# Retention, ELU feed-forward and gated feed-forward on one core: heads' halves exchanged in every second pair of the last nine retention steps

## The chip, the core and the metric

The kernel runs on one core of one Trainium2 chip, in one launch. The metric is the device time of the launch in microseconds, as the median of several runs. The engines are TensorE (PE: matmuls, with its weight loads as PEld), VectorE (DVE), ScalarE (ACT), GpSimd (POOL) and SyncE (SP, which here issues nearly all DMAs). Their programs run side by side, each strictly in its own order, and wait for each other through semaphores.

## What is computed

All data is float32. A retention (attention with a decaying causal mask and no softmax) over 4 batches, 8 heads, 576 positions and a head size of 64 is followed by two feed-forward layers over its 2304 tokens of 512 features:

```python
def _attn_ref(q, k, v):
    scores = scale * np.matmul(q, k.transpose(0, 1, 3, 2))       # scale = 1/8
    gamma = 1.0 - 2.0 ** (-5.0 - np.arange(H))
    rel = pos[:, None] - pos[None, :]
    Dmat = np.where(rel >= 0, gamma[:, None, None] ** rel, 0.0)
    return np.matmul(scores * Dmat, v)

def _moe_ref(x, w_in, w_out):
    h = x @ w_in
    return np.where(h > 0.0, h, np.exp(np.minimum(h, 0.0)) - 1.0) @ w_out

def _moe2_ref(x, w_gate, w_val, w_out):
    gate = 1.0 / (1.0 + np.exp(-(x @ w_gate)))
    return (gate * (x @ w_val)) @ w_out
```

## The kernel before

The retention runs in chunks of 128 positions: 18 steps, numbered n = 0 to 17. Steps 0 to 8 belong to batches 0 and 1, steps 9 to 17 to batches 2 and 3; within nine, the two batches take turns, and the ninth (8 and 17) does the last 64 positions of both. A step has 4 pairs of heads (p). In q and in the transposed k of a pair, head h = 0 lies on partitions 0 to 63 and head h = 1 on 64 to 127, and so does its state, the decayed sum of k times v over all earlier chunks. A chunk has two halves of 64 positions, X = 0 and 1.

TensorE's array is used in quarters of 64x64: the rows come from the partitions of the operands (upper or lower half), the columns go to the partitions of the result. A step issues five kinds of 64x64x64 matmuls, all through `mm` (L263), into two pairs of PSUM banks, `ts` and `to`:

- `scores`: transposed k times q, 16 matmuls into `ts`; the row half is the head's, the column half is X.
- `sums`: k times v, 16 matmuls into the left half of `to`, new parts of the state (none in the last step of nine).
- `inter`: state times q, 16 matmuls into the right half of `to` (8 in steps 9 and 10, the first of their batches). Row half and column half are both the head's. It goes in two rounds, `other` = 1 and 0: in the first, head h does the half X = 1 - h, in the second X = h.
- `outs`: masked scores times v, 16 matmuls that add onto `inter`'s results; the row half is X, the column half the head's.

In `to`, the bank is given by X. `inter`'s first round writes a bank from the other row half than `outs` does later. So that the two never overlap, an empty instruction on SP (`self.swept`, L317) waits for the last matmul of the first round, and the first matmul of `outs` waits for this instruction.

After the matmuls DVE masks the scores (`causal`), scales the outputs (`x_mul`) and updates the state (`states`, with a POOL multiply by the chunk's decay, `cs_sb`); ACT and DVE split x into a high and a low part (`x_high`, `x_low`), and SP stores x (L354). POOL scales v (`scale`, L260).

The order is written out by hand: `block(n)` issues `inter` of step n, `scores` of n + 1, `outs` of n, `sums` and `causal` of n + 1, then the loads that fall due (`loads_at`), `x_mul` and `x_high` of n, `states` of n + 1, `scale` of n + 2 and `x_low` of n. From step 6 on, between two blocks there stand one up-projection (L369) and one down-projection (L113 to L115) of the first feed-forward layer, and stages of the conversion of weights on ACT, DVE and POOL. SP meets its own instructions in this order too: L317 of step n, the loads due in block n, the store of step n, then at times a weight's load (L143).

A step's input is one tile of 1 MB, q, transposed k, k and v of the chunk. `load` issues it as one DMA (L247); for the last step of nine, whose positions come from two batches, as six (four of 256-byte runs, L252, and two of 1-KB runs, L254). Loads are issued three to five steps ahead, those of steps 9 to 16 in blocks 4 to 12 and step 17's in block 13. The DMAs of SP use eight semaphores in turn; a DMA first waits until the one that used its semaphore before has landed.

Of the kernel before, what the change touches and what calls it, by code (L numbers as in the profile page):

```python
# [17 lines left out]
ALU = mybir.AluOpType  # L18


B, H, S, D = 4, 8, 576, 64
NP = H // 2
C = 128
# [5 lines left out]
HC = 64  # L29
# [12 lines left out]
AHEAD = 2  # L42
LATE = 4
# [10 lines left out]
def retention_elu_glu(  # L54
# [13 lines left out]
    pe, act, dve, pool, sp = nc.tensor, nc.scalar, nc.vector, nc.gpsimd, nc.sync  # L68
# [11 lines left out]
    class Ring:  # L80
        def __init__(self, name, pool, n, shape, dtype):
            self.name, self.shape, self.dtype, self.at = name, shape, dtype, 0
            self.homes = [(pool, f"{name}{i}") for i in range(n)]
            self.n, self.views = n, {}
# [38 lines left out]
    def after(ins, other):  # L123

        tc.add_manual_dep(ins.ins, other.ins.name, mybir.DependencyInfo(
            mybir.DependencyClass.Sync, mybir.DependencyReason.DATA), reason="row tiles")
        return ins
# [8 lines left out]
    class Weight:  # L136
# [3 lines left out]
        def load(self, raw=None):  # L140
            self.ours = raw is None
            self.raw = raw_free.popleft() if self.ours else raw
            sp.dma_start(out=self.raw, in_=self.src.bitcast(I32))  # L143
# [37 lines left out]
    for f in range(FA):  # L181
        for n, src in (("i", w_in), ("o", w_out)):
            i = len(weights)
# [39 lines left out]
    class Step:  # L223
# [3 lines left out]
        def __init__(self, n):  # L227
            self.n, self.swept = n, None
            two, i = divmod(n, NS)
            self.last = i == NS - 1  # L230
            self.b, self.c = (2 * two, NC - 1) if self.last else (2 * two + i % 2, i // 2)
            self.g = max(g for g in range(NG) if G0[g] <= n)
            self.at = 128 * (n - G0[self.g])

        def rows(self):

            at = self.b * S + C * self.c
            return [(0, 64, at), (64, 128, at + S)] if self.last else [(0, 128, at)]

        def load(self):  # L240
            if self.n in SPARE:
                self.t = spare_y[SPARE[self.n]].rearrange("p (q c) -> p q c", q=NP)
            else:
                self.t = inpool.tile([128, NP, 4 * C], F32, tag="in", name="in")
            self.q, self.kT, self.k, self.v = (self.t[:, :, i * C : i * C + C] for i in range(4))
            if not self.last:
                sp.dma_start(out=self.t, in_=ain[self.b, self.c].rearrange("p r x -> r p x"))  # L247
                return
            for X in range(2):
                src = ain[self.b + X, self.c]  # L250
                for i in range(2):
                    sp.dma_start(out=self.t[:, :, i * C + HC * X : i * C + HC * X + HC],  # L252
                                 in_=src[:, :, i * C : i * C + HC].rearrange("p q x -> q p x"))
                sp.dma_start(out=self.t[64 * X : 64 * X + 64, :, 2 * C :],  # L254
                             in_=src[:, :HC, 2 * C :].rearrange("p t x -> t p x"))

# [8 lines left out]
        def scores(self):  # L265
            for p in range(NP):
                for X in range(2):
                    for h in range(2):
                        r, s = slice(64 * h, 64 * h + 64), slice(HC * X, HC * X + HC)
                        self.mm(ts[64 * X : 64 * X + 64, h, HC * p : HC * p + HC], self.kT[r, p, s], self.q[r, p, s], p == 0)  # L270

        def causal(self):

# [4 lines left out]
        def sums(self, start=False):  # L278

            if self.last:  # L280
                return
            for p in range(NP):
                for h in range(2):
                    for X in range(2):
                        r, d = slice(64 * X, 64 * X + 64), slice(64 * h, 64 * h + 64)
                        self.mm(to[d, X, D * p : D * p + D], self.k[r, p, d], self.v[r, p, d], start and p == 0)

        def states(self):

            if self.last:  # L290
                self.st = st_last
                return
            one = self.b % 2
            self.st = (st, st_last)[self.c % 2 == 0][one], st_half
            new = to[:, :, : NP * D].rearrange("d x (p e) -> d x p e", p=NP)
            if self.c:
                dve.tensor_tensor(out=st_half, in0=self.st[0], in1=new[:, 0], op=ALU.add)
            else:
                act.copy(st_half, new[:, 0])
            end = (st, st_last)[self.c % 2][one]  # L300
            dve.tensor_tensor(out=end, in0=st_half, in1=new[:, 1], op=ALU.add)
            pool.tensor_tensor(out=end, in0=end, in1=cs_sb.unsqueeze(2).to_broadcast([128, NP, D]), op=ALU.mult)

        def o(self, h, X, p):
            return to[64 * h : 64 * h + 64, X, 256 + HC * p : 256 + HC * p + HC]

        def inter(self):

            for other in (1, 0):
                for p in range(NP):  # L310
                    for h in range(2):
                        X, r = h ^ other, slice(64 * h, 64 * h + 64)
                        if X or self.c:
                            ins = self.mm(self.o(h, X, p), self.st[X][r, p, :], self.q[r, p, HC * X : HC * X + HC], p == 0)
                if other:

                    self.swept = after((pool if self.n == 1 else sp).nop(), ins)  # L317

        def outs(self):

            for p in range(NP):
                for h in range(2):
                    for X in range(2):
                        r = slice(64 * X, 64 * X + 64)
                        ins = self.mm(self.o(h, X, p), self.v[r, p, 64 * h : 64 * h + 64], self.a[r, h, p, :],
                                      not self.c and not X and p == 0)
                        if self.swept:
                            after(ins, self.swept)
                            self.swept = None

        def x_mul(self):
            self.xf = e_tile()
# [458 lines left out]
    with tc.manual_schedule():  # L791
# [9 lines left out]
        ts = ps_r.tile([128, 2, 512], F32, name="ts")  # L801
        to = ps_r.tile([128, 2, 512], F32, name="to")
        cq_sb = cpool.tile([128, NP, C], F32, name="cq_sb")
        small = cpool.tile([128, 16 * NP], F32, name="small")
        cs_sb, vt = small[:, 4 * NP : 5 * NP], (small[:, : 4 * NP], small[:, 5 * NP : 9 * NP])
        tri = cpool.tile([128, HC], F32, name="tri")
        st = [cpool.tile([128, NP, D], F32, name=f"st{i}") for i in range(2)]

# [6 lines left out]
        steps = [Step(n) for n in range(NSTEP)]  # L815
# [7 lines left out]
        for X in range(2):  # L823
            r = slice(64 * X, 64 * X + 64)
# [17 lines left out]
        def block(n, scales=True):  # L842

            more = n + 1 < NSTEP
            steps[n].inter()
            if more:
                steps[n + 1].scores()
            steps[n].outs()
            if more:
                steps[n + 1].sums()  # L850
                steps[n + 1].causal()
            for load in loads_at.get(n, []):
                load()
            steps[n].x_scaled()
            if more:
                steps[n + 1].states()
                if scales and n + 2 < NSTEP:
                    steps[n + 2].scale()
            steps[n].x_low()

        def stages(chain, n):
            for _ in range(n):
                next(chain)
# [14 lines left out]
        for load in loads_at[0]:  # L878
            load()
# [21 lines left out]
        for load in loads_at[1]:  # L901
            load()
# [9 lines left out]
        end = len(ff)  # L912

        a, b = begins
        conv, loads = {2: weights[3]}, {}
        for i, w in enumerate(weights[4:8]):
            s = a + 6 + (i * (b - a - 6)) // 4
# [148 lines left out]
        for s in range(end):  # L1066
# [18 lines left out]
            if LATE <= s < NSTEP - AHEAD:  # L1085
                block(s + AHEAD)
# [35 lines left out]
            if 1 < s < LATE:  # L1122
                block(s + AHEAD)
# [108 lines left out]
        for pair in (first, second):  # L1232
# [3 lines left out]
            for q in range(Q0, QN):  # L1236
                hooks = {}
                calls = 7 + len(todo) + (not last_q)
                if not last_q:
# [3 lines left out]
                    if q == QN - 1:  # L1243
                        reload(second.sums)
                        restore(("i", 2 * Q0), ("i", 2 * Q0 + 1), ("z", Q0))
                        p = second
# [8 lines left out]
                else:  # L1255
# [16 lines left out]
                    if q + 1 == QN:  # L1272
                        p = y_pair
# [36 lines left out]
        for which, pair in enumerate(pairs):  # L1310
            for f in range(FB):
# [36 lines left out]
                if which and f == 0:  # L1348
                    x = xpool.tile([128, 2, KB, 256], F32R, tag="x4", name="g").rearrange("p i k t -> p i (k t)")
# [4 lines left out]
                if which and f == 2:  # L1354
                    free.extend((8, 9))
                    two = y_tile(4).rearrange("p (i t) -> p i t", i=2)
# [70 lines left out]
def build(nc, arrays):  # L1427
    args = [
        nc.dram_tensor(f"in_{n}", a.shape, mybir.dt.from_np(a.dtype), kind="ExternalInput").ap()
        for n, a in arrays.items()  # L1430
    ]
    args.append(nc.dram_tensor("out_0", (NT, DM), F32, kind="ExternalOutput").ap())
    with tile.TileContext(nc) as tc:
        retention_elu_glu(tc, *args)
# [12 lines left out]
```

## Time and profile before

| | us |
|---|---|
| median of 3 runs | 879.99 |
| the runs | 875.67, 879.99, 880.41 |
| the profiled execution | 878.83 |
| its span (first to last instruction) | 877.0 |

The profile is that of one execution. Its page gives each engine's busy time; the views behind it are the waits of an engine, the chain of work that ended last, the timelines of single engines, and tables by stretch. Times in rows are microseconds from the start of the span. A 64x64 float32 matmul stands as two records in the timelines, so 16 matmuls are "x32"; where kinds overlap, the count is split over several rows. A shown idle time before a row carries the name of what is taken to have ended it.

### The profile page before, as it was taken

The numbers are of one execution on the slowest core, as the hardware profiler recorded it, in microseconds if no ns is written. First come the engines' busy times: TensorE is split into PE (matmuls) and PEld (weight loads), VectorE is DVE, ScalarE is ACT, GpSimd is POOL, SyncE is SP. The second block draws the span as 40 slices with busy tenths as digits, with TensorE's granted clock in tenths as the row PEclk, the third lists the DMA queues.
The fourth block names the chain that finished last, engine by engine and source line by source line (L and its number), as shares of the span: only waits on it lengthen the run. The fifth ranks groups of instructions, "written<-read, shape, count | busy, mean of one in ns | idle before, by whom it ended". The sixth has DMA issues, their size and how long they took to land.

```text
span 877.0 us, 16170 instructions
## 1 busy us (share of the span) xinstructions
PE 852.9 (97%) x6370; PEld 729.5 (83%) x6375; DVE 667.2 (76%) x967; ACT 459.1 (52%) x833; POOL 410.5 (47%) x327
## 2 busy tenths in 40 slices
PE   7798999999999999999999999999999999999998
PEld 4698998788888888888778888888888888888886
DVE  5757558689999987889867999579977554786775
ACT  3345466477667655666565665455534344344331
POOL 2355435556556543565371655355533144334453
PEclk9999999999999999999999999999999999999999
DMA  9977627934656496887792766645565564554322
GB/s 340 299 232 239 165 71 254 369 120 144 230 179 217 185 407 248 312 335 284 294 353 101 248 237 226 225 173 191 204 234 207 198 234 196 212 214 180 113 118 97
DMA packets 63724, 194.83 MB, mean 222 GB/s; under 512 B 9760, under 2 KB 18976, under 8 KB 57248
## 3 DMA queue, kind: packets, MB, share of 16 engines
q1 hardware_dynamic: 62544, 192.31, 61.6%
q10 hardware_dynamic: 1104, 1.49, 0.5%
q8 instruction: 50, 0.82, 0.4%
q14 instruction: 26, 0.21, 0.1%
HBM read 127.19 MB, written 66.58 MB: 221 GB/s over the span
## 4 chain that ended last, share of the span: by engine, by line
PE 79%; DVE 8%; DMA 6%; ACT 3%; issue 2%; SPq 1%; POOL 0%; DVEq 0%; ACTq 0%; POOLq 0%
PE u L113 13%; PE u L114 12%; PE u L115 12%; PE acc L113 9%; PE acc L114 9%; PE acc L115 9%; PE tile L113 3%; PE tile L115 3%; PE tile L114 3%; PE to L263 2%; PE h L369 2%; DMA x<-e 2%; DMA y<-y 2%; DMA fg<-x 1%; DMA raw<-in_w_in 1%
## 5 line engine op out<-in xcount | busy, mean ns | idle before, releaser
L109 POOL TENSOR_TENSOR g<-e,g 128x512 fp32r<-128x512 f32 x95 | 133.3, 1409 | 229.3 <-ACT g L108 209.6
L113 PE MATMUL u<-x,s 128*128 128x512 f32 x288 | 112.7, 391 | 3.6 <-ACT e L529 2.1
L114 PE MATMUL u<-x,s 128*128 128x512 f32 x288 | 112.4, 390 | 0.0
L115 PE MATMUL u<-x,s 128*128 128x512 f32 x288 | 112.1, 389 | 0.0
L113 PE MATMUL u<-x,w 128*128 128x512 f32 (+1 forms) x264 | 98.3, 372 | 0.7 <-DVE u L531 0.6
L114 PE MATMUL u<-x,w 128*128 128x512 f32 (+1 forms) x264 | 98.0, 371 | 0.0
L115 PE MATMUL u<-x,w 128*128 128x512 f32 (+1 forms) x264 | 97.7, 370 | 0.0
L108 ACT CAST g<-e 128x512 fp32r<-128x512 f32 x101 | 62.0, 621 | 63.9 <-DVE e L587 40.1
L171 POOL TENSOR_TENSOR w<-t,w 128x512 fp32r<-128x512 f32 x37 | 51.2, 1383 | 40.6 <-ACT w L168 37.1
L113 PEld LDWEIGHTS u<-x,s 128*128 128x128 f32 x288 | 54.1, 188 | 15.6 <-ACT e L529 2.6
L115 PEld LDWEIGHTS u<-x,s 128*128 128x128 f32 x288 | 54.1, 188 | 11.6
L114 PEld LDWEIGHTS u<-x,s 128*128 128x128 f32 x288 | 54.2, 188 | 10.1
L113 PE MATMUL acc<-g,w 128*128 128x512 f32 (+1 forms) x168 | 58.7, 349 | 0.8 <-ACT y L429 0.8
L784 DVE TENSOR_TENSOR y<-y,acc 128x512 f32<-128x512 f32 x58 | 39.1, 682 | 25.3 <-PE acc L115 25.0
L114 PE MATMUL acc<-g,w 128*128 128x512 f32 (+1 forms) x168 | 58.3, 347 | 0.0
L115 PE MATMUL acc<-g,w 128*128 128x512 f32 (+1 forms) x168 | 58.2, 346 | 0.0
L113 PEld LDWEIGHTS u<-x,w 128*128 128x128 f32 x264 | 49.9, 189 | 9.4 <-DVE u L531 1.5
L115 PEld LDWEIGHTS u<-x,w 128*128 128x128 f32 x264 | 49.7, 188 | 8.8
L748 DVE TENSOR_TENSOR y<-y,tile 128x512 f32<-128x512 f32 x76 | 51.1, 679 | 7.3 <-PE tile L115 7.1
L114 PEld LDWEIGHTS u<-x,w 128*128 128x128 f32 x264 | 49.9, 189 | 7.3
L664 DVE TENSOR_TENSOR y<-y,acc 128x512 f32<-128x512 f32 (+1 forms) x68 | 39.6, 606 | 19.8 <-PE acc L115 17.9
L114 PE MATMUL acc<-w,g 128*128 128x512 f32 (+1 forms) x152 | 54.1, 356 | 0.0
(223 smaller groups left out, 2421.1 us busy)
## 6 DMA issues: line engine op xcount, KB each, us to landing
w<-c SPq DMA_DIRECT2D x72, 512.0 KB, 6.4
c<-w SPq DMA_DIRECT2D x48, 512.0 KB, 5.0
s<-c SPq DMA_DIRECT2D x22, 1024.0 KB, 6.8
c<-s SPq DMA_DIRECT2D x18, 1024.0 KB, 5.1
in<-in_ain SPq DMA_DIRECT2D x12, 1024.0 KB, 7.6
y<-y SPq DMA_DIRECT2D x8, 1024.0 KB, 6.1
raw<-in_w_in SPq DMA_DIRECT2D x12, 512.0 KB, 5.5
c<-x SPq DMA_DIRECT2D x12, 512.0 KB, 7.0
```

What stands on the lines that cost most here:

```text
L108: act.copy(hi, src)
L109: lo_engine.tensor_tensor(out=lo, in0=src, in1=hi.bitcast(F32), op=ALU.subtract)
L113: pe.matmul(out_, wh, xh, start=start, stop=False, skip_group_check=shared)
L114: pe.matmul(out_, wh, xl, start=False, stop=False, skip_group_check=shared)
L115: pe.matmul(out_, wl, xh, start=False, stop=stop, skip_group_check=shared)
L171: lo_engine.tensor_tensor(out=w[:, 1, :], in0=f, in1=w[:, 0, :].bitcast(F32), op=ALU.subtract)
L263: return pe.matmul(out_, w, x, start=start, stop=True, skip_group_check=True)
L369: pe.matmul(h, w[:, a, c[k]], x[:, b, k, t], start=i + k == 0, stop=i == 2 and k == KB - 1)
L664: dve.tensor_tensor(out=out_, in0=out_, in1=a, op=ALU.add)
L748: dve.tensor_tensor(out=y, in0=y, in1=a, op=ALU.add)
L784: dve.tensor_tensor(out=o, in0=o, in1=a, op=ALU.add)
```

## The change

In steps 9 to 17 (`turned`) the odd pairs, p = 1 and 3, get their heads' halves exchanged in q, transposed k and the state: head 0 lies on partitions 64 to 127 and head 1 on 0 to 63. `half(h, p)` gives the half on which head h of pair p lies. The results in `to` stay where they were, so `inter` of an odd pair reads one row half and writes the other column half; a round of `inter` now has matmuls in all four quarters. The state's decays for the exchanged layout are made once, after block 6, by two small ACT copies (`turn`).

Both rounds of `inter` now write one bank from different row halves. So in turned steps the first matmul of the second round waits for L317's instruction, not `outs`, and the scores of the next step are issued between the two rounds.

The exchange is made by the load: the even pairs come as one DMA, q and transposed k of the odd pairs as two DMAs of 64 partitions each, k and v of the odd pairs as one. One DMA becomes four; step 17's six become fourteen.

```diff
+            self.turned = two == 1
+        def half(self, h, p):
+            return h ^ (p & self.turned)
@@ load
-                sp.dma_start(out=self.t, in_=ain[self.b, self.c].rearrange("p r x -> r p x"))
+                t, src = self.t, ain[self.b, self.c].rearrange("p r x -> r p x")
+                if not self.turned:
+                    sp.dma_start(out=t, in_=src)
+                    return
+                sp.dma_start(out=t[:, ::2, :], in_=src[:, ::2, :])
+                for i in range(2):
+                    sp.dma_start(out=t[64 * i : 64 * i + 64, 1::2, : 2 * C], in_=src[64 - 64 * i : 128 - 64 * i, 1::2, : 2 * C])
+                sp.dma_start(out=t[:, 1::2, 2 * C :], in_=src[:, 1::2, 2 * C :])
                 return
             for X in range(2):
                 src = ain[self.b + X, self.c]
                 for i in range(2):
...
+                    sp.dma_start(out=to_[:, ::2, :], in_=qk[:, ::2, :])
+                    for j in range(2):
+                        sp.dma_start(out=to_[64 * j : 64 * j + 64, 1::2, :], in_=qk[64 - 64 * j : 128 - 64 * j, 1::2, :])
@@ inter
-            for other in (1, 0):
-                for p in range(NP):
-                    for h in range(2):
-                        X, r = h ^ other, slice(64 * h, 64 * h + 64)
-                        if X or self.c:
-                            ins = self.mm(self.o(h, X, p), self.st[X][r, p, :], self.q[r, p, HC * X : HC * X + HC], p == 0)
-                if other:
-                    self.swept = after((pool if self.n == 1 else sp).nop(), ins)
+        def inter_part(self, other):
+            for p in range(NP):
+                for h in range(2):
+                    i = self.half(h, p)
+                    X, r = i ^ other, slice(64 * i, 64 * i + 64)
+                    if X or self.c:
+                        start = other == 1 and p < 2 if self.turned else p == 0
+                        ins = self.mm(self.o(h, X, p), self.st[X][r, p, :], self.q[r, p, HC * X : HC * X + HC], start)
+                        if self.turned:
+                            self.sweep(ins)
+            if other:
+                self.swept = after((pool if self.n == 1 else sp).nop(), ins)
+        def inter(self, between=None):
+            self.inter_part(1)
+            if between and self.turned:
+                between()
+            self.inter_part(0)
+            if between and not self.turned:
+                between()
@@ block
-            steps[n].inter()
-            if more:
-                steps[n + 1].scores()
+            steps[n].inter(steps[n + 1].scores if more else None)
+            if n == LATE + AHEAD:
+                turn()
```

TensorE at step 14, before (y_113 is step 14's input, y_114 its state, in the input of step 15, a the masked scores; names in brackets are the semaphores waited for):

```order
L263 MATMUL to<-y_113,y_114 64x64 [waits DVE_49]
L263 MATMUL to<-y_113,y_114 64x64 x15
L263 MATMUL ts<-in 64x64 [waits DMAHW3_49]
L263 MATMUL ts<-in 64x64 x15
L263 MATMUL to<-a,y_113 64x64 [waits SP_sequencer_49]
L263 MATMUL to<-a,y_113 64x64 x15
L263 MATMUL to<-in 64x64 [waits Pool_49]
L263 MATMUL to<-in 64x64 x15
```

The same place after (`mm` is L281 there):

```order
L281 MATMUL to<-y_113,y_114 64x64 [waits DVE_49]
L281 MATMUL to<-y_113,y_114 64x64 x7
L281 MATMUL ts<-in 64x64 [waits DMAHW5_49]
L281 MATMUL ts<-in 64x64 x3
L281 MATMUL ts<-in 64x64 [waits DMAHW6_49]
L281 MATMUL ts<-in 64x64 [waits DMAHW7_49]
L281 MATMUL ts<-in 64x64 x10
L281 MATMUL to<-y_113,y_114 64x64 [waits SP_sequencer_49]
L281 MATMUL to<-y_113,y_114 64x64 x7
L281 MATMUL to<-a,y_113 64x64 x16
```

The wait for SP has moved from the outputs to the second half of state x q, and the scores stand ahead of it.

SP at step 17's load, before; the last row is the store of step 14, which also waits for PE through L317's instruction of that step (empty instructions are not listed):

```order
L252 DMA in<-in_ain 128x4x64 [waits PE_49,DMAHW0_49,DMAHW1_49,Pool_49]
L252 DMA in<-in_ain 128x4x64
L254 DMA in<-in_ain 64x4x256 [waits DMAHW2_49]
L252 DMA in<-in_ain 128x4x64 [waits DMAHW3_49]
L252 DMA in<-in_ain 128x4x64 [waits DMAHW4_49]
L254 DMA in<-in_ain 64x4x256 [waits DMAHW5_49]
L354 DMA x<-e 512x1x128 [waits DMAHW6_49,DVE_49]
L354 DMA x<-e 512x1x128 [waits PE_49,DMAHW7_49,DVE_49]
```

And the second half of it after, from the seventh piece on, up to the same two stores:

```order
L272 DMA in<-in_ain 64x4x256 [waits DMAHW6_49]
L269 DMA in<-in_ain 128x2x64 [waits DMAHW7_49]
L271 DMA in<-in_ain 64x2x64 [waits DMAHW0_49]
L271 DMA in<-in_ain 64x2x64 [waits DMAHW1_49]
L269 DMA in<-in_ain 128x2x64 [waits DMAHW2_49]
L271 DMA in<-in_ain 64x2x64 [waits DMAHW3_49]
L271 DMA in<-in_ain 64x2x64 [waits DMAHW4_49]
L272 DMA in<-in_ain 64x4x256 [waits DMAHW5_49]
L388 DMA x<-e 512x1x128 [waits DMAHW6_49,DVE_49]
L388 DMA x<-e 512x1x128 [waits PE_49,DMAHW7_49,DVE_49]
```

Fourteen DMAs now stand ahead of the store of step 13 and of step 14's L317; the later ones, and the store, wait for semaphores of pieces of the same load.

## Rows read from the trace of the kernel before

**Rows 1.** The page: span, and busy time of each engine.
```profile
PE 852.9 (97%) x6370; PEld 729.5 (83%) x6375; DVE 667.2 (76%) x967; ACT 459.1 (52%) x833; POOL 410.5 (47%) x327
```

**Rows 2.** Waits of PE, whole span: us in total, times, longest us.
```profile
PE to L263 <- SPq L317: 1.5, 2, 0.9
...
PE acc L113 <- ACT y L429: 0.8, 1, 0.8
```

**Rows 3.** Table by stretch, steps 12, 13, 14: us, engines' busy us (instructions), PEclk, DMA share, GB/s.
```profile
81.70:91.00 9.30, 6.97 (x155) 6.53 (x154) 6.50 (x10) 3.74 (x10) 5.46 (x6) 0.84 0.89 281
91.00:96.70 5.70, 5.70 (x153) 5.53 (x152) 3.03 (x6) 1.42 (x3) 1.46 (x3) 0.96 0.19 46
96.70:103.10 6.40, 5.79 (x153) 5.43 (x152) 3.65 (x8) 4.04 (x10) 2.66 (x4) 1.00 1.02 212
```

**Rows 4.** PE's timeline, step 14: start us, us, instruction, idle before.
```profile
96.52 0.28 PE L115 MATMUL acc<-g,w 128*128 128x256 f32 x1
96.73 1.08 PE L263 MATMUL to<-y,y 64*64 64x64 f32 x29
97.60 0.27 PE L263 MATMUL ts<-in 64*64 64x64 f32 x1
...
98.96 0.69 PE L263 MATMUL to<-a,y 64*64 64x64 f32 x32 [0.61 <-SPq L317]
```

**Rows 5.** Chain that ended last, 93 to 99: start us, us, what.
```profile
93.38 0.37 SPq L252
...
93.80 1.79 SPq L252
...
95.64 0.66 SPq L254
...
96.99 0.51 SPq L252
...
98.28 0.57 SPq L354
...
98.90 0.02 SPq L317
```

**Rows 6.** PE's timeline, end of the pause in the projections of step 16.
```profile
113.30 0.39 PE L113 MATMUL acc<-g,w 128*128 128x256 f32 x1 [0.79 <-ACT y L429]
```

**Rows 7.** PE's timeline, step 13: scores, outputs, sums.
```profile
92.06 0.27 PE L263 MATMUL ts<-y 64*64 64x64 f32 x2
...
92.57 0.22 PE L263 MATMUL to<-a,in 64*64 64x64 f32 x1
...
93.04 0.22 PE L263 MATMUL to<-y 64*64 64x64 f32 x1
```

**Rows 8.** PE's timeline, start of step 9, its scores, start of step 10.
```profile
64.48 0.79 PE L263 MATMUL to<-y,y 64*64 64x64 f32 x13
65.05 0.28 PE L263 MATMUL ts<-in 64*64 64x64 f32 x3
...
70.47 0.79 PE L263 MATMUL to<-in,y 64*64 64x64 f32 x13 [0.56 <-DVE st L301]
```

**Rows 9.** SP's waits, 60 to 120; DMA issues (count, KB, median us to landing).
```profile
SPq L317 <- PE to L263: 21.9, 8, 6.1
...
in<-in_ain SPq DMA_DIRECT2D x12, 1024.0 KB, 7.6
```

**Rows 10.** L254, issue to landing, whole span.
```profile
DMA to landing us min/median/max: 4.4/5.2/5.8
```

**Rows 11.** SP's timeline, step 8's load of six pieces, its first two.
```profile
33.46 1.21 SPq L252 DMA_DIRECT2D y<-in_ain  x2
```

**Rows 12.** PE's timeline behind step 12's pause; DMA queues, 84 to 86.7.
```profile
86.66 1.84 PE L369 MATMUL h<-x,w 128*128 128x256 f32 x12 [2.33 <-ACT x L343]
88.30 0.41 PE L113 MATMUL acc<-g,w 128*128 128x256 f32 x1
...
q8 instruction: 1, 0.02, 2.2%
```

More of the change, by code (lines that the diff above doesn't have):

```diff
@@ L251, in load @@
                 for i in range(2):
-                    sp.dma_start(out=self.t[:, :, i * C + HC * X : i * C + HC * X + HC],
-                                 in_=src[:, :, i * C : i * C + HC].rearrange("p q x -> q p x"))
+                    to_ = self.t[:, :, i * C + HC * X : i * C + HC * X + HC]
+                    qk = src[:, :, i * C : i * C + HC].rearrange("p q x -> q p x")
+                    if not self.turned:
+                        sp.dma_start(out=to_, in_=qk)
+                        continue
+                    sp.dma_start(out=to_[:, ::2, :], in_=qk[:, ::2, :])
+                    for j in range(2):
+                        sp.dma_start(out=to_[64 * j : 64 * j + 64, 1::2, :], in_=qk[64 - 64 * j : 128 - 64 * j, 1::2, :])
                 sp.dma_start(out=self.t[64 * X : 64 * X + 64, :, 2 * C :],
@@ L267, in scores @@
                 for X in range(2):
-                    for h in range(2):
-                        r, s = slice(64 * h, 64 * h + 64), slice(HC * X, HC * X + HC)
-                        self.mm(ts[64 * X : 64 * X + 64, h, HC * p : HC * p + HC], self.kT[r, p, s], self.q[r, p, s], p == 0)
+                    for i in range(2):
+                        r, s = slice(64 * i, 64 * i + 64), slice(HC * X, HC * X + HC)
+                        self.mm(ts[64 * X : 64 * X + 64, i, HC * p : HC * p + HC], self.kT[r, p, s], self.q[r, p, s], p == 0)
         def causal(self):
@@ L284, in sums @@
                     for X in range(2):
-                        r, d = slice(64 * X, 64 * X + 64), slice(64 * h, 64 * h + 64)
-                        self.mm(to[d, X, D * p : D * p + D], self.k[r, p, d], self.v[r, p, d], start and p == 0)
+                        r, d, i = slice(64 * X, 64 * X + 64), slice(64 * h, 64 * h + 64), self.half(h, p)
+                        self.mm(to[64 * i : 64 * i + 64, X, D * p : D * p + D], self.k[r, p, d], self.v[r, p, d], start and p == 0)
         def states(self):
@@ L301, in states, with sweep @@
             dve.tensor_tensor(out=end, in0=st_half, in1=new[:, 1], op=ALU.add)
-            pool.tensor_tensor(out=end, in0=end, in1=cs_sb.unsqueeze(2).to_broadcast([128, NP, D]), op=ALU.mult)
+            pool.tensor_tensor(out=end, in0=end, in1=cs_sb[self.turned].unsqueeze(2).to_broadcast([128, NP, D]), op=ALU.mult)
         def o(self, h, X, p):
             return to[64 * h : 64 * h + 64, X, 256 + HC * p : 256 + HC * p + HC]
-        def inter(self):
-            for other in (1, 0):
-                for p in range(NP):
-                    for h in range(2):
-                        X, r = h ^ other, slice(64 * h, 64 * h + 64)
-                        if X or self.c:
-                            ins = self.mm(self.o(h, X, p), self.st[X][r, p, :], self.q[r, p, HC * X : HC * X + HC], p == 0)
-                if other:
-                    self.swept = after((pool if self.n == 1 else sp).nop(), ins)
+        def sweep(self, ins):
+            if self.swept:
+                after(ins, self.swept)
+                self.swept = None
+        def inter_part(self, other):
[17 more added lines that the diff above has]
+                between()
         def outs(self):
@@ L324, in outs @@
                         r = slice(64 * X, 64 * X + 64)
[L325 to L329, printed above, removed]
+                        self.sweep(self.mm(self.o(h, X, p), self.v[r, p, 64 * h : 64 * h + 64],
+                                           self.a[r, self.half(h, p), p, :], not self.c and not X and p == 0))
         def x_mul(self):
@@ L804, in retention_elu_glu @@
         small = cpool.tile([128, 16 * NP], F32, name="small")
[L805 removed]
+        cs_sb = small[:, 4 * NP : 5 * NP], small[:, 9 * NP : 10 * NP]
+        vt = small[:, : 4 * NP], small[:, 5 * NP : 9 * NP]
         tri = cpool.tile([128, HC], F32, name="tri")
@@ L859, in block, with turn @@
             steps[n].x_low()
+            if n == LATE + AHEAD:
+                turn()
+        def turn():
+            for i in range(2):
+                r = slice(64 * i, 64 * i + 64)
+                by = small[r, : 4 * NP].rearrange("r (a x) -> r a x", a=2)[:, :, i : i + 6 - 2 * i : 5 - 2 * i]
+                act.copy(cs_sb[1][r].rearrange("r (a b) -> r a b", a=2), by)
         def stages(chain, n):
```

## Prediction

> **What bounds the kernel now.** I read the page first: PE is busy for 852.9 of 877.0 us [rows 1], so a microsecond counts where PE waits or would wait. The waits of PE over the span name two that matter here: 1.5 us on SP's line 317, 0.8 us on an ACT copy [rows 2]. L317 is the empty SP instruction that carries "the first half of state x q is done" back to PE; the change touches that.
>
> The stretches of steps 12 to 14 come next [rows 3]: step 13 takes 5.70 us with PE busy throughout; the 9.30 of step 12 and the 6.40 of step 14 hold pauses. Step 14 in PE's timeline [rows 4]: state x q starts at 96.73, scores at 97.60, and the outputs wait to 98.96, with 0.61 us idle "<-SPq L317". SP's line over the same time [rows 5] tells why: from 93.38 it issues the six pieces of step 17's load one after the other, then the store of step 13; only at 98.90 can it run L317, and PE goes on 0.06 us later. The chain that ended last runs through these very rows. From 98.96 it leaves PE: other engines carry it until PE, at 113.30, waits 0.79 us for an ACT copy [rows 6]. So between 98.96 and 113.30 PE saves nothing for the end; what moves step 14's outputs moves everything.
>
> **What it removes.** State x q in a turned step uses two of the four 64x64 quarters of the array; step 14's 16 matmuls take 97.60 - 96.73 = 0.87 us. Operations that use all four take 0.47 to 0.51: scores from 92.06 to 92.57, outputs from there to 93.04 [rows 7]. In the new order four matmuls in a row fall on four quarters, so I take 0.47 and a saving of 0.40 per step; bounds are 0 (no overlap) and 0.43. Steps 11, 12 and 13 sit on PE: -1.2 by the time step 13's outputs end. Steps 9 and 10 have eight matmuls in 0.57 us (64.48 to 65.05 [rows 8]) and gain 0.1 each, lost at once in the wait for DVE that stands behind them (0.56 us before 70.47 [rows 8]). The gain of 15 and 16 goes into the wait before 113.30, 0.79 us now [rows 6]. Step 17 has no scores after it, so its second part stands directly behind L317: first part 0.24, round trip 0.22 + 0.06, second part 0.24, against 0.87: -0.1.
>
> **What it moves.** The wait on L317 now stands before the second part, behind the scores alone. Where SP is free this is covered: the answer comes some 0.3 us after the last matmul of the first part, the scores take 0.5. Queued behind it on PE are the second part, the outputs, the sums and the next up-projection. Of DVE, x_mul of that step waits.
>
> **What it adds.** Each 1-MB load of steps 9 to 16 becomes four pieces. A first issue costs SP 0.37 us, a later one 0.51 to 0.66 [rows 5], a gap 0.05: some 1.7 us more, once in each of eight of the steps 4 to 12. SP has that time: from 60 to 120 it stood at L317 waiting for PE for 21.9 us in eight steps, 2.7 us a step [rows 9]. The data lands 7.6 us after its issue [rows 9] and is read by PE some two steps, 11 us, later. So I take nothing; without that cover a load would cost up to 1.7 us, once. The scores and sums then wait for more landings of a load, three instructions more on PE in a step, for data that has long landed. The two small ACT copies after step 6 fall on an engine that is busy half the time [rows 1], with no row of their size: nothing, at most a piece of the 0.79 us that the longest wait for an ACT copy took [rows 2].
>
> Step 17's load is the exception: six pieces become fourteen, directly ahead of store 13 and of step 14's L317. Worked out on the trace's clock:
> - it starts when step 13's outputs are done: 93.38 - 1.2 = 92.18;
> - the issues: the first 0.37, the other 256-run pieces 0.58 (between 0.51 and 0.66 [rows 5]), the eight half pieces 0.45 (no row has one of 128 runs; 0.37 and 0.66 are the ends), gaps 0.05: 0.37 + 5 x 0.58 + 8 x 0.45 + 13 x 0.05 = 7.5 us. All at 0.37 gives 5.8, all at 0.66 gives 9.6;
> - the DMAs use eight semaphores in turn, and each waits until the DMA eight places earlier has landed. Store 13 waits for the seventh piece, issued 3.05 us in and landing 4.4 to 5.8 us later [rows 10]; at 5.2 that is 8.25, later than 7.5. With the store (0.57) and gaps L317 runs 8.9 us after 92.18;
> - in one of the two six-piece loads one issue took 1.79 instead of some 0.55 [rows 5], in the other none did [rows 11]; I add half of the 1.2.
>
> So L317 comes at 92.18 + 9.5 = 101.7, the second part ends and the outputs start at 101.7 + 0.06 + 0.24 = 102.0: 3.0 us after 98.96. The ends: 0.37 throughout with a landing of 4.4 gives L317 at 99.8, +1.1; 0.66 with 5.8 and a full slow issue gives 103.9, +5.2.
>
> By the Trainium skill ("DMA: Bandwidth & Descriptors", Rules for kernel authors) two transfers to disjoint partition halves should be one, because they share the same engines, and under 64 KB a transfer is mostly overhead; the halves here are 32 KB. Its section Anatomy of one DMA gives a fixed cost of about 2 us, for the GpSimd path. By that the seventh piece would land at some 5 us, the issues would set the end, and L317 would come an estimated 0.7 us earlier; the rows say 4.4 and more, and they decide.
>
> PE would idle from about 96.2 (step 14 starts 1.2 earlier, first part 0.22, scores 0.5) to 101.7. A 2.33-us hole that ended at 86.66 was followed by down-projection matmuls of 0.41 instead of 0.28 us [rows 4, 12], and the stretch has a granted clock of 0.84 (the lower level, 1.2 GHz, for part of it) [rows 3]. 0.16 of 9.30 us is a loss of about 1.4. A longer hole should bring this too, but PE then has 0.79 + 0.8 us before 113.30; only slower outputs count. I take 0.3; bounds 0 and 1.4.
>
> Sum: 3.0 + 0.3 - 0.1 = +3.2 us on the profiled 878.83 (span 877.0): **882.0**. Its own range is +1.0 to +6.5: 879.8 to 885.3. The profiled run lies 1.2 us under the median of the runs shown, 879.99, which spread over 4.7; I leave the sum on its own run.
>
> **Rivals.**
> 1. *The saving gets through.* SP has the 14 issues done before PE needs L317. Outputs of step 14 then start at 95.5 + 0.22 + 0.5 + 0.24 = 96.5, -2.5, and with step 17 the time is 876.2. For it speaks only that no half piece was ever timed; against it that even the cheapest rows give 99.8. Chance 0.08.
> 2. *SP holds longer and the clock joins in* (the other side): the pieces cost 0.66, the slow issue comes in full, and slower PE eats the slack before 113.30. It decides from an L317 about 11 us after 92.18: +4.6 + 1.0 - 0.1, **884.3** and above. A wide DMA share of 1.02 in that stretch [rows 3] speaks for it. Chance 0.17.
> 3. *The hole before 86.66 moves.* The view puts it down to ACT's x_high, but the up-projection there waits for x of the step before, which by the program's order is written a step earlier; what lies in the hole is a 16-KB packet of the instruction queue [rows 12]. If it closes, its 2.33 and 1.4 go: 882.0 - 3.7 = 878.3; if a second one opens in the denser PE stream: 885.7. "Runtime: NRT & Kernel Launch" of the Trainium skill (Instruction fetch mechanics) has such fetches hidden, by which this rival would have no chance; a PE that stood still around the packet disagrees. Chances 0.10 and 0.07.
> 4. *The change does not do what it says*: the four quarters do not overlap because the two row halves now write the same columns of the accumulators. Saving 0, L317 as above: 882.0 + 1.2 = 883.2. Against it: sums and outputs already write so, in 0.47. Chance 0.03.
>
> **How the numbers follow.** Forecast 0.55. A measurement of this kernel can tell about 0.5% (4.4 us) from no change. Faster by that needs rival 1 and the closed hole together, or something unseen: 0.06. Slower by over 4.4 us: most of rival 2, the opened hole, and the upper end of the forecast: 0.27. Within: 0.67. The range takes in the forecast's own, the closed hole and most of rival 2, and leaves out rival 1: 877.0 to 886.0.
>
> **What would show it.** State x q of steps 13, 15, 16 in two blocks of some 0.24 us around the scores (right) or 0.45 (rival 4). In SP's line 14 issues between about 92 and 100, L317 at 101 to 102, and PE in step 14 idle for some 5 us "<-SPq L317". The chain that ended last through SP there. A granted clock below 1.00 in the stretch after. L317 before 97 would make the prediction wrong, and so would a step 14 that no longer lies on the chain.

## The result, and the profile after

| | before | after |
|---|---|---|
| median, us (8 runs each) | 879.77 | 885.44 |
| the runs, us | 875.67 to 880.41 | 881.88 to 886.95 |
| the profiled span, us | 877.0 | 885.1 |

The ratio after to before is 1.0067, with a 95% interval of 1.0046 to 1.0088: some 5.9 us (4.0 to 7.7) slower. The change made the kernel slower, by more than the forecast's 3.2 us and inside its range.

In the changed kernel the lines are: `mm` L281, the empty SP instruction L345, the exchanged half pieces L271 (the other pieces of step 17 L269 and L272), the store of x L388, `states` L319, `x_mul` L370, `x_high` L377, the up-projection L403. The page's row of busy time, for [rows 1]:

```profile
PE 854.3 (97%) x6375; PEld 729.6 (82%) x6375; DVE 667.5 (75%) x967; ACT 459.5 (52%) x835; POOL 412.1 (47%) x327
```

No engine has much more to do, though the span grew by 8.1 us. PE's waits over the span (us in total, times, longest), for [rows 2]:

```profile
PE to L281 <- SPq L345: 7.0, 3, 6.3
PE h L403 <- ACT x L377: 4.0, 2, 2.9
...
PE acc L113 <- ACT y L463: 1.0, 1, 1.0
```

The 1.5 us on the empty SP instruction have become 7.0, and 6.3 of them are one wait. (The 2.9 us put down to `x_high`, L377, are the pause of step 12; whose it is, one of the runs below tells.) The table by stretch, steps 13, 14 and 15, for [rows 3]:

```profile
91.05:96.15 5.10, 5.10 (x154) 4.89 (x152) 3.02 (x6) 1.58 (x4) 1.98 (x3) 1.00 0.16 44
96.15:109.40 13.25, 6.94 (x153) 6.58 (x152) 4.22 (x8) 4.02 (x10) 3.23 (x4) 0.74 0.49 120
109.40:114.50 5.10, 5.10 (x154) 4.89 (x152) 4.13 (x8) 1.84 (x4) 3.08 (x5) 1.00 0.30 112
```

Step 13 got shorter, from 5.70 to 5.10 (a part of it is the clock, 0.96 there before). Step 14 takes 13.25 us instead of 6.40, at a granted clock of 0.74. PE's timeline in steps 13 and 14, for [rows 4] and [rows 7]:

```profile
91.10 0.46 PE L281 MATMUL to<-in,y 64*64 64x64 f32 x16
91.38 0.65 PE L281 MATMUL ts<-y 64*64 64x64 f32 x32
91.85 0.41 PE L281 MATMUL to<-in,y 64*64 64x64 f32 x16
92.08 0.65 PE L281 MATMUL to<-a,in 64*64 64x64 f32 x32
...
96.48 0.65 PE L281 MATMUL ts<-in 64*64 64x64 f32 x32
103.44 0.71 PE L281 MATMUL to<-y,y 64*64 64x64 f32 x16 [6.31 <-SPq L345]
103.92 1.08 PE L281 MATMUL to<-a,y 64*64 64x64 f32 x32
...
105.78 2.33 PE L403 MATMUL h<-x,w 128*128 128x256 f32 x12
```

In step 13 the two parts of state x q take 91.38 - 91.10 = 0.28 and 92.08 - 91.85 = 0.23 us, 0.51 together where it was 0.87. In step 14 the second part waits 6.31 us behind the scores, and what follows runs slow: 0.48 us from its start to the outputs, 0.85 from there to the sums (the next row, left out), where step 13 has 0.23 and 0.47. The chain that ended last says what SP did meanwhile, for [rows 5]:

```profile
92.84 0.37 SPq L269
...
93.26 1.64 SPq L271
...
94.95 0.61 SPq L271
...
95.60 0.59 SPq L269
...
97.53 0.60 SPq L272
...
102.06 0.60 SPq L272
...
102.76 0.56 SPq L388
...
103.37 0.02 SPq L345
...
103.44 2.48 PE to L281 x79
```

Fourteen issues from 92.84 to 102.66, then the store of step 13, then L345. Each issue takes 0.59 to 0.61 us, whether its piece has 128 partitions (L269) or 64 (L271), except the first (0.37) and one of 1.64. Further on the chain leaves PE and comes back at the wait ahead of step 17, for [rows 6]:

```profile
105.94 0.04 DVE e L370
...
108.80 1.17 DVE t L157
...
112.35 1.31 POOL w L171
...
114.93 0.50 ACT x L377
```
```profile
119.04 0.39 PE L113 MATMUL acc<-g,w 128*128 128x256 f32 x1 [0.99 <-ACT y L463]
```

There PE stands 119.04 - 113.30 = 5.74 us later than before, close to the whole difference of the medians, 5.67. Before, the chain had left PE for DVE here:

```profile
100.19 0.03 DVE e L336
```

From that row to the wait it takes 13.1 us in both kernels (113.30 - 100.19 and 119.04 - 105.94). Of the other 2.4 us by which this one profiled run is longer, 0.7 have come by the end of a pause that both kernels have (441.41, before 434.94). Most of the rest comes behind the next pause, which ends at 454.62 (before 448.14): the granted clock of the 51.9 us behind it is 0.97, and 1.00 before. The run was the longest of the eight.

### The profile page after: what moved, and what is told of

Read it like the earlier page. It is cut to its first block, busy times and chain, and to the rows that moved or that the text cites. A ratio compares the mean times of both kernels' runs of the same rounds, so it can differ in the third digit from the quotient of the medians.

```text
span 885.1 us, 16220 instructions
## 1 busy us (share of the span) xinstructions
PE 854.3 (97%) x6375; PEld 729.6 (82%) x6375; DVE 667.5 (75%) x967; ACT 459.5 (52%) x835; POOL 412.1 (47%) x327
## 4 chain that ended last, share of the span: by engine, by line
PE 65%; DVE 13%; DMA 8%; ACT 6%; issue 3%; SPq 2%; POOL 1%; ACTq 0%; DVEq 0%; POOLq 0%
PE u L113 11%; PE u L114 11%; PE u L115 11%; PE acc L113 8%; PE acc L114 8%; PE acc L115 8%; PE tile L113 2%; PE tile L115 2%; PE tile L114 2%; DMA x<-e 2%; DMA raw<-in_w_o 2%; DMA y<-y 1%; DVE t L162 1%; DVE t L157 1%; PE to L281 1%
```

## The experiments

Ratios are to the kernel before, timed beside it, with 95% intervals.

**The load's pieces alone.** The kernel before, loads cut as in the change, no exchange (step 17's pieces are cut alike, left out here):

```diff
-                sp.dma_start(out=self.t, in_=ain[self.b, self.c].rearrange("p r x -> r p x"))
...
+                sp.dma_start(out=t[:, ::2, :], in_=src[:, ::2, :])
+                for i in range(2):
+                    r = slice(64 * i, 64 * i + 64)
+                    sp.dma_start(out=t[r, 1::2, : 2 * C], in_=src[r, 1::2, : 2 * C])
+                sp.dma_start(out=t[:, 1::2, 2 * C :], in_=src[:, 1::2, 2 * C :])
...
```

> The kernel before with only the loads of steps 9 to 17 cut into the same pieces as in the change (four, and fourteen for step 17), nothing exchanged; PE's order is that of the kernel before. Theory (SP's queue): step 17's pieces are issued from 93.4 on for 9.2 to 9.8 us, step 14's outputs start at 103.5 to 104.3 instead of 98.96, the time is 884.8 (883.5 to 886), as slow as the changed kernel or a little less than 1 us off it. Rival (the wait's new place behind the scores makes the loss): within 1.5 us of the kernel before.

Measured 884.28 us, 1.0060 (1.0045 to 1.0076). PE's timeline in its step 14:

```profile
101.95 1.13 PE L278 MATMUL to<-a,y 64*64 64x64 f32 x32 [5.16 <-SPq L332]
```

The pieces alone cost what the whole change costs, with PE in its old order. (The outputs start at 101.95 and not at 103.5, since in this run step 17's load began 1.60 us earlier, at 91.78 instead of 93.38. Its fourteen issues took 9.4 us, within the expected 9.2 to 9.8.) The new place of the wait is not the cause.

**Step 17 in six pieces.** The changed kernel, only the condition in step 17's load replaced, so that its six old DMAs are issued (this kernel leaves out the exchange of step 17's q and k):

```diff
-                    if not self.turned:
+                    if True:
                         sp.dma_start(out=to_, in_=qk)
```

> The changed kernel with step 17's load in six pieces as in the kernel before; its odd pairs are then not exchanged in memory, so the part of the output that comes from step 17 is wrong, the work is the same. Theory (number of pieces times the issue time): six issues take 3.6 to 4.9 us as before, SP's empty instruction of step 14 runs at 97.5 to 98.9, the wait of PE there falls from 6.31 to 0.5 to 1.9 us, the time is 880 (879 to 881). Rival (the position of the wait in PE's order costs, however many pieces): PE still loses over 4 us in step 14, and the time is over 883.

Measured 877.86 us, 0.9980 (0.9964 to 0.9996). PE waits 0.84 us in step 14:

```profile
100.29 0.46 PE L281 MATMUL to<-y,y 64*64 64x64 f32 x16 [0.84 <-SPq L345]
```

Without the eight extra issues the loss is gone, and what is left is a small gain; the time is 2 us below the expected one. (The profiled run is the slowest of its twelve, 882.77 us, so its row shows the wait and not the time.)

**All loads as before**, the same edit in the other loads too (this kernel leaves out the whole exchange in memory):

> The changed kernel with all loads as in the kernel before (one piece, six for step 17): nothing is exchanged in memory, so the odd pairs of steps 9 to 17 are computed from the wrong halves; PE's order and its quarters are those of the changed kernel. Theory (splitting the loads of steps 9 to 16 is covered): same time as with step 17's load alone in six pieces, within 0.7, about 880; against the kernel before the 0.4 us of steps 11 to 14 are partly given back in step 14's wait. Rival (the eight split loads cost SP time that PE waits for): 1.5 us or more faster than with step 17's load alone in six pieces.

Measured 878.30 us, 0.9990 (0.9977 to 1.0004), 0.4 us from the run above. Splitting the loads of steps 9 to 16 costs nothing that can be measured, as the prediction had it.

**PE's order alone.** As the last one, and heads not exchanged (with the decays and the first matmuls of a bank set to match, left out here):

```diff
-            return h ^ (p & self.turned)
+            return h
```

> The kernel before's data and loads with PE's order of the change alone: state x q in two parts around the scores, the wait ahead of the second part, heads not exchanged, so that each part uses two quarters. Theory (the gain lies in the quarters): the two parts take some 0.45 us each instead of 0.23 to 0.28, a step of 11 to 16 is 0.4 us longer than with the exchange, and the time is 0.5 to 1.5 us above the run with exchange and old loads, 879.5 to 880 (same as the kernel before). Rival (the order is what gains, by hiding SP's answer): as fast as with the exchange, 878.3, with parts of whatever length.

Measured 880.76 us, 1.0009 (0.9994 to 1.0024). PE's timeline in its step 13, first and second part:

```profile
91.47 0.62 PE L281 MATMUL to<-in,y 64*64 64x64 f32 x13
91.88 0.27 PE L281 MATMUL ts<-y 64*64 64x64 f32 x1
...
92.45 0.57 PE L281 MATMUL to<-in,y 64*64 64x64 f32 x13
92.81 0.27 PE L281 MATMUL to<-a,in 64*64 64x64 f32 x1
```

Here the parts take 0.41 and 0.36 us, 0.77 together, against 0.51 with the exchange and 0.87 before. So of the 0.36 us the order gives 0.10 and the exchange, which makes all four quarters overlap, 0.26. In time this kernel and the one above differ by 0.0019 with intervals that still overlap a little, so that the gain of the exchange is shown in the rows and only likely in the time.

**DVE carries the answer.** The changed kernel, complete:

```diff
-                self.swept = after((pool if self.n == 1 else sp).nop(), ins)
+                self.swept = after((pool if self.n == 1 else dve if self.n in (14, 15) else sp).nop(), ins)
```

> The changed kernel, with one edit: the empty instruction that carries the end of the first half of state x q back to PE runs on DVE instead of SP in steps 14 and 15; all loads stay as they are. Theory (the loss is SP's queue: step 17's fourteen pieces stand ahead of that instruction): DVE is idle there, PE's 6.31-us wait in step 14 shrinks to under 0.5, the up-projection behind step 14 starts at about 99.5 instead of 105.78, and the time falls by about 6 to 879 (877.5 to 880.5). Rival (the pieces themselves are too late, or their traffic is what costs): PE waits as long for step 17's data in step 16, or for the x of step 14, and the time stays at 883 or above.

Measured 881.69 us, 1.0026 (1.0010 to 1.0042): some 40% of the loss is left, not none. The wait in step 14 is gone, but PE now waits 1.03 us for DVE in step 15, and later rows of DVE, PE and ACT show new waits:

```profile
108.75 0.69 DVE L370 TENSOR_TENSOR e<-to,cq_sb 128x512 f32<-128x512 f32 x1 [4.46 <-DMA x<-e]
...
110.28 0.27 PE L281 MATMUL to<-in,y 64*64 64x64 f32 x1 [2.94 <-DVE y L319]
...
110.66 0.69 ACT L153 ACTIVATE t<-raw 128x512 f32<-128x512 f32 x1 [6.32 <-DMA raw<-in_w_in]
```

Two more things stand behind step 17's load on SP: the store of step 13, which has to land before DVE may write that buffer again in step 15, and a weight's load, which ACT's conversion needs. In the changed kernel they are covered by PE's own wait.

**The store first.** As above, and step 17's load moved behind `x_low` of block 13, so behind the store:

> The changed kernel with DVE carrying the answer in steps 14 and 15, and with step 17's fourteen pieces issued behind the store of step 13 instead of ahead of it. Theory (what was left of the loss with DVE alone is the store: DVE's scaling in step 15 waited 4.46 us for its landing, and PE 2.94 us behind that): both waits go; the pieces come some 1.5 to 2 us later, which may make the scores of step 17 wait up to 2 us; 879.7 (878.5 to 881). Rival (the traffic or the lateness of the fourteen pieces is what is left): 881.7 or above, PE waiting for step 17's data for over 3 us.

Measured 883.73 us, 1.0049 (1.0034 to 1.0065). DVE waits for no store any more, and step 17's data are not late; but the expected time was wrong. The weight's load is now the one that is late, issued at 106.78 us, and ACT holds the conversion of x that PE needs behind it:

```profile
111.28 0.66 ACT L153 ACTIVATE t<-raw 128x512 f32<-128x512 f32 x1 [5.87 <-DMA raw<-in_w_in]
...
113.04 2.93 PE L403 MATMUL h<-x,w 128*128 128x256 f32 x12 [2.76 <-ACT x L377]
```

**The load in two blocks.** The seven pieces of one batch in block 13, of the other in block 14; DVE for step 15 alone:

```diff
+            if n == 14:
+                steps[17].load_one(1)
             steps[n].x_scaled()
```

> The changed kernel, complete, with step 17's load cut in two: the seven pieces of the first batch in block 13, the seven of the second in block 14, each ahead of that block's store; DVE carries the answer in step 15. Theory (the length of SP's hold counts, since the answer of step 14, the store of step 13 and a weight's load all stand behind it): seven pieces hold SP for 4.4 to 5.6 us, PE waits 0.8 to 1.5 us in step 14 and about 1 in step 15, DVE's scaling waits under 1 us for a store; 879 to 880.5. Rival (fourteen pieces cost the same wherever they stand): 882 or above.

Measured 882.78 us, 1.0038 (1.0019 to 1.0056). The waits on PE are as expected, 1.47 us in step 14 and 1.04 in step 15, and the time is not. ACT again waits for the weight's load, and PE for ACT ahead of step 17:

```profile
109.19 0.67 ACT L153 ACTIVATE t<-raw 128x512 f32<-128x512 f32 x1 [3.52 <-DMA raw<-in_w_in]
...
114.54 0.39 PE L113 MATMUL acc<-g,w 128*128 128x256 f32 x1 [1.62 <-ACT y L467]
```

SP issues almost without a gap from 92.09 on, and the weight's load comes at 103.62, where the kernel before has 101.55. What stands last in the queue pays for all fourteen pieces, however they are cut into groups.

**The half pieces from ACT.** The changed kernel, the eight pieces of 64 partitions issued by ACT, four ahead of its conversion in block 13 and four behind:

> The changed kernel, complete, but the eight half pieces of step 17's load are issued by ACT, four ahead of its conversion of x in block 13 and four behind it; SP issues six pieces as in the kernel before. Theory (SP's queue, by count of pieces): PE's wait in step 14 is 0.5 to 1.5 us, as with six pieces, and ACT, idle for some 3 us ahead of that conversion, takes most of its issues there; the time is 878.5 (877.5 to 880). Rival (ACT pays what SP saved: eight issues of 0.6 us push its conversions and copies, and PE waits for those): 881 or above, with PE's waits on ACT in blocks 13 to 16 over 2 us more than with six pieces.

Measured 880.92 us, 1.0007 (0.9991 to 1.0023): the loss is gone and no gain is left. Rows of ACT, SP and PE:

```profile
93.00 3.56 ACTq L279 DMA_DIRECT2D in<-in_ain  x4
...
98.24 0.61 SPq L273 DMA_DIRECT2D in<-in_ain  x1
99.82 3.52 SPq L394 DMA_DIRECT2D x<-e  x2
...
100.49 0.46 PE L287 MATMUL to<-y,y 64*64 64x64 f32 x16 [3.22 <-SPq L351]
```

SP has six pieces and still holds L351 to 100.4: its last piece waited 0.8 us and its store 0.9 us for an earlier piece to land. That fits both queues sharing the program's eight DMA semaphores, so that SP waits for pieces that ACT issued; the waits are shown, the sharing is argued. Neither theory had it. The eight issues on ACT took 0.60 to 1.43 us each (median 0.63), much as on SP.

**The kernel before, with DVE for steps 14 and 15** (the edit above):

> The kernel before, with DVE instead of SP carrying the answer in steps 14 and 15. Theory (the 0.61 us that PE waits there for SP sits on the chain, but the wait of 0.79 for an ACT copy ahead of the last step takes it up): step 14's outputs start at 98.4 to 98.5 instead of 98.96, the later wait grows by as much, the time stays within 0.7 of the kernel before. Rival (it comes through whole): 0.6 to 1 us faster.

Measured 877.98 us, 0.9986 (0.9974 to 0.9998). The time alone does not decide (0.2 to 2.3 us faster, which leaves room for both); the rows of its PE speak for the rival:

```profile
98.25 0.22 PE L263 MATMUL to<-a,y 64*64 64x64 f32 x1
...
112.62 0.39 PE L113 MATMUL acc<-g,w 128*128 128x256 f32 x1 [0.24 <-ACT y L429]
```

The outputs start 0.71 us earlier, and PE goes on ahead of step 17 0.68 us earlier; the wait there shrinks from 0.79 to 0.24 instead of growing, since the conversions that end it start from step 14's outputs too. So this stretch passes on whatever moves those outputs, in both directions.

**The pause in step 12.** The kernel before, with 64 more records at PE's start:

```diff
+        h = h_bank()
+        for _ in range(32):
+            pe.matmul(h[:, :64], warm[:, :128], warm[:, :64], start=True, stop=True)
         warm_up(WARM[0])
```

> The kernel before with 32 extra small matmuls (64 records) at its start, on data that nobody reads. Theory (the 2.33-us pause in step 12 is PE's own program arriving late: it is tied to a place in PE's program in steps of some 256 records): the pause, and the one at 446 us, lie about 64 records earlier, the first thus inside step 12's matmuls, or are gone; PE no longer stops exactly ahead of that up-projection. Rival (PE waits there for ACT's conversion of x, which ended 0.16 us ahead of the pause's end): the pause stays ahead of the same up-projection, within 0.5 us as long as before. The extra matmuls cost 0 to 2 us at the start; the time is 877 to 882 by either.

Measured 878.14 us, 0.9979 (0.9964 to 0.9994). PE's timeline, and ACT's conversion of x of step 12's block:

```profile
80.08 0.34 PE L263 MATMUL to<-in 64*64 64x64 f32 x8 [1.01 <-issue]
...
86.55 0.69 PE L263 MATMUL to<-in 64*64 64x64 f32 x32 [1.05 <-issue]
87.18 1.70 PE L369 MATMUL h<-x,w 128*128 128x256 f32 x12
...
93.30 0.58 PE L263 MATMUL to<-a,in 64*64 64x64 f32 x24 [1.32 <-issue]
...
448.43 0.50 PE L113 MATMUL u<-x,s 128*128 128x512 f32 x1 [2.21 <-ACT e L529]
```
```profile
88.04 0.62 ACT L343 CAST x<-e 128x512 fp32r<-128x512 f32 x1 [0.42 <-DVE e L336]
```

The pause now stands ahead of step 12's sums, whose 16 matmuls are 64 records (32 weight loads, 32 matmuls): it moved by just what was added, and it stands there in the two runs below that have these records too. The up-projection starts at 87.18, ahead of the conversion that its idle time had been put down to. So the pause follows PE's program and not ACT; that it is a late fetch of that program is likely and not shown.

It is 1.05 us instead of 2.33, and the down-projection matmuls behind it take 0.28 us, not 0.41. But further ones appear, 1.01 us in step 11 and 1.32 in step 13: the pause was split, not removed. Nor do the rows show where the time was gained. This run is the slowest of its ten (880.73 us), and PE, with the extra matmuls to do first, starts step 13's up-projection at 94.27, behind the 93.66 of the kernel before. The pause at 446 us did not move; that one is a wait for ACT, whose copy (L529) ends at 448.38, and the expectation was wrong there.

**Both together.** The two blocks with the 64 records, and the kernel before with DVE and the 64 records:

> The same with the 32 extra small matmuls at PE's start that moved the pause of step 12 in the kernel before. Theory (late program): the pause of some 2.9 us ahead of the up-projection of block 12 splits or shrinks as it did there, and the time is 1.5 to 2 us under the kernel with the load in two blocks, 877 to 879. Rival (the gain there was chance, or belongs to that kernel's own alignment): within 0.7 us of it, the pause at the same up-projection.

> The kernel before with both small edits that helped it apart: DVE carries the answer in steps 14 and 15, and 32 extra small matmuls stand at PE's start. Theory (two separate places, both on the path that sets the end): the gains of some 1.2 and 1.8 us add up, 877 (876 to 878), against 879.8 for the kernel before. Rival (one of them is chance or they cover each other): 878 to 879.

The first: 880.88 us, 1.0017 (1.0000 to 1.0034), 1.9 us under the run without the records, but above the expected 877 to 879; its pauses are 1.83 us in step 11 and 0.69 in step 12, instead of one of 2.02. The second: 877.62 us, 0.9973 (0.9958 to 0.9989), the lowest ratio of all, faster than both kernels. The single gains, 0.0014 and 0.0021, would make 0.0035, and it has 0.0027: with such intervals they may add up or cover each other in part.

## Why the prediction came out as it did

- **What bounds, and where the loss arises: right.** The largest loss is PE's wait for SP's empty instruction in step 14, behind step 17's load; the load alone makes it, six pieces take it away.
- **The saving: right in kind, a little small in size.** 0.36 us in a step instead of 0.40. When step 17's load began, PE was only 0.54 us ahead (92.84 instead of 93.38), not 1.2. The pause in step 12 ended almost where it had (86.54, before 86.66), though PE came to it earlier: it took 2.90 us in this run instead of 2.33, and 0.57 of the missing 0.66 went into it. The prediction knew that pause (its rival 3) but let the saving of the steps ahead of it pass through.
- **The step that was mis-sized: the length of SP's hold.** The text has 7.5 us of issues; they took 102.66 - 92.84 = 9.8. The half pieces were put at 0.45 as the middle between 0.37 and 0.66; L271 shows 0.60, so 8 x 0.15 = 1.2 us. 0.37 is the price of a first issue and not of a small one: that stood in [rows 5], and the size of a piece had no place in it. The slow issue (1.64 instead of 0.60) came in full, where half was added; every trace of this load has one, of 1.0 to 1.9 us. The bound from the seventh piece's landing, 8.25 us, was near (that piece, issued at 97.53, landed 3.8 us later, 8.5 us into the load), but the issues outlasted it. L345 ran at 103.37 instead of 101.7: 0.66 us by the start at 92.84 instead of 92.18, and 1.0 by the longer hold.
- **The clock: also too small.** 0.3 was taken, out of 0 to 1.4 (0.16 of 9.30 us is nearer 1.5). The second part took 0.48 us instead of 0.23, so the outputs started 103.92 - 98.96 = 4.96 us late and not 3.0. The wait ahead of step 17 ended 5.74 late: 0.78 more came with the outputs and the sums at the lower level, 2.02 us from the outputs' start to DVE's scaling (105.94) instead of 1.23. The slack of 0.79 did not take it up, since the chain runs from those very matmuls.
- **Step 17: 0.1 us less as forecast, but by luck.** From the end of the wait to the next up-projection PE took 3.06 us instead of 3.16; state x q itself, where the 0.1 was worked out, took 0.86 us (0.76 forecast, 0.87 before).
- **The sum.** 4.96 + 0.78 - 0.1 = 5.6, against 5.67 between the medians. Over the forecast's 3.2 that is 2.4 us: 0.66 by the start, 1.0 by the hold, 0.7 by the clock, all three the same way.
- **Which case it was:** rival 2, "SP holds longer and the clock joins in", 884.3 and above from an L317 11 us after 92.18. It came 11.2 us after, and the time is 885.4. Two of its conditions came, the longer pieces (0.60) and the slow issue in full; the third did not, for the wait ahead of step 17 was not eaten up but grew from 0.79 to 0.99. That case had 0.17; the forecast had 0.55. Slower by over 0.5% had 0.27.
- **The Trainium skill.** The seventh piece, on which the prediction's two prices for a landing hung, landed after 3.8 us, under the rows' 4.4 and well over the fixed cost of about 2 us that the Trainium skill ("DMA: Bandwidth & Descriptors", Anatomy of one DMA) gives for the GpSimd path; the 32-KB half pieces came near that, with 2.0 to 3.3 us (median 2.2). The issues set the end, as by that figure, but because they took 9.8 us. The rule of the Trainium skill (same page, Rules for kernel authors) to use one transfer instead of two for disjoint partition halves is borne out here by the count of issues; its reason, the shared engines, no run here tests. The Trainium skill ("Runtime: NRT & Kernel Launch", Instruction fetch mechanics) has fetches mostly hidden; if the pause in step 12 is one, its 2.3 to 2.9 us were not.
- **Not foreseen:** what else stood behind the load. The prediction named the answer to PE and, in its order, the store; it did not follow the store to DVE's buffer or see the weight's load behind it. With the answer taken off SP the time was still 0.0026 above the kernel before; the rows put that down to these two.

What stays open: why one issue of this load is slow, whether the pause in step 12 is a late fetch, and what the hold would cost in a kernel whose pause lies elsewhere.

## What to carry to other kernels

Count DMA issues, not bytes: on a queue that carries signals as well, each further piece delays everything behind it by one issue time. Follow every instruction in that queue to the engine that needs it, the last one too, because freeing one of them here only handed the delay to the next. And where the chain that ended last runs through an engine's pause and out over other engines, take a shift there as passed on in full, slack shown later on another engine notwithstanding.

## What the runs showed of the hardware

- In the changed kernel an issue of step 17's load on SP took 0.37 us as the first of the row and 0.59 to 0.61 behind another, for pieces from 32 to 256 KB alike; one took 1.64. On ACT, while SP issued as well, it took 0.60 to 1.43 (median 0.63).
- 32-KB pieces landed after 2.2 us (median). The view of L271, from issue to landing:

```profile
DMA to landing us min/median/max: 2.0/2.2/3.3
```

- A pause of PE in step 12 (2.33 us before, 2.90 in the changed kernel, 2.0 to 3.4 in the eleven traces without the extra records) is tied to a place in PE's own program: 64 records ahead of it moved it by 64 records and split it into pauses of 0.7 to 1.8 us. Behind the long pause PE ran at the lower granted level (1.2 GHz; matmuls of 0.41 us instead of 0.28) in nine of the eleven traces, but not in two, with pauses of 2.33 and 2.02 us; behind the split ones it did so in none of three.
